# Two attention blocks with a gate: mask products of the maxima issued ahead, and three small tasks moved by one group

## The chip, the cores and the metric

The kernel runs on one core of a Trainium2 chip. The metric is the device time of one execution in microseconds (us). A core has five engines that run side by side: TensorE (in the profile PE, and PEld for its weight loads), VectorE (DVE), ScalarE (ACT), GpSimd (POOL) and SyncE (SP), which issues the transfers. TensorE writes its products into eight banks of a small memory, PSUM, from which VectorE and ScalarE read them.

## The reference

Two attention blocks read the same input of 2048 positions and 512 columns, with 32 heads of 16 columns each, and a gate mixes their outputs.

```python
def _A_ref(x, wq, wk, wv, wo, beta):          # 4 chunks of 512 positions
    ...
    for s in range(N):
        qs, ks, vs = q[:, :, s], k[:, :, s], v[:, :, s]
        logits = jnp.einsum("bhqd,bhkd->bhqk", qs, ks) * scale + mask   # causal inside the chunk
        p = _softmax(logits, axis=-1)
        a_dot = jnp.einsum("bhqk,bhkd->bhqd", p, vs)
        pq = phi(qs)
        num = jnp.einsum("bhld,bhde->bhle", pq, M)
        den = jnp.einsum("bhld,bhd->bhl", pq, z)[..., None] + 1e-6
        outs.append(g * (num / den) + (1.0 - g) * a_dot)
        M = M + jnp.einsum("bhld,bhle->bhde", phi(ks), vs)
        z = z + ...
    ...
def _B_ref(x, wqkv, wo):                      # every position sees all 2048
    scores = jnp.einsum("bhqd,bhkd->bhqk", q, k) * (Dh ** -0.5)
    p = _softmax(scores, axis=-1)
    o = jnp.einsum("bhqk,bhkd->bhqd", p, v)
    ...
g = _sigmoid((x * gate_w).sum(-1, keepdims=True))
return g * a + (1 - g) * b
```

The softmax of both blocks subtracts the maximum of a row, and the kernel computes these maxima in passes of their own.

## The kernel before

**Units and rounds.** Work is cut into units: a unit is four heads and one chunk of 512 queries. Block A has 32 (numbers 0 to 31), block B has 32 (32 to 63). After a first stage of about 400 us (projections, the memory of block A, first maxima) come 32 rounds. Round `k` works on unit `32 + k` of B and unit `k` of A.

**Slots.** A round has 37 groups, here called slots: `n` from 0 to 31 for B (16 key tiles, two heads at a time), 32 to 36 for A. All instructions of a slot are issued in the order in which the loop over `n` calls the functions, and each engine runs its own in that order. A slot holds:

- `t_group`: products of keys and queries (line 503, on half of the rows of TensorE each, two side by side) into two of the three banks TB0, TB1 and MB, the least recently used first; then two exponentials on ScalarE (line 509), and in A's slots a masking of the diagonal on GpSimd (line 512).
- the tasks of `plan`: maxima of units that come later. A task writes logits into SBK (two pairs of banks, taken in turn by `rot("s", SBK)`), and VectorE takes the maximum over the keys.
- `pvs`: products of probabilities and values (`pv`, line 525) into the one bank PVB, for groups issued earlier. In slot 33 the last of them for B's unit, and behind it a copy of the bank by `fin_copy` (on ScalarE for B, line 534); in slot 34 the first of A's unit, into the same bank. In slot 36 two calls for A, in slot 0 of the next round A's last one and a copy on VectorE (line 532).
- in some slots `beside`, with the finishing of earlier units. In slot 36 of every even round from 8 on, `out_split` (ScalarE line 584, GpSimd line 585). In slot 1 of the rounds from 9 on, `out_mm` (24 products, line 591).

**The tasks.** Each round computes the maxima of one later unit of B in 32 tasks (`s_b`: two products, line 449, reduction in line 451) and of the next unit of A in 6 (`s_a`, in the order of `ST_A`). A's tasks take the query tiles 3, 3, 2, 2, 1, 0; the first four have one pair of heads each (one part), the last two have both (two parts, in the columns 0 to 255 and 256 to 511 of a bank). A part is one product of queries and keys for each of the two row halves (line 427), followed by two small products for each half that add the causal mask (line 431: `crows` as weights, `cmask` streaming, 128 and 64 columns wide). The reductions are in lines 435 and 437.

**Where the tasks stand.** `spread` puts one B task into each of the slots 20 to 31 and 36 of a round and 1 to 19 of the next; A's tasks stand in the slots 32 to 36 and, the sixth, in slot 0 of the next round. So slot 36 has two tasks, A's fifth and one of B. `m_chain` in slot 21 reads the maxima.

Of the kernel before, what the change touches and what calls it, by code (L numbers as in the profile page):

```python
# [23 lines left out]
NT = SEQ // 128  # L24
# [3 lines left out]
S_FIRST = 10  # L28
S_LAST = 10
# [4 lines left out]
def gated_mix_kernel(ctx, tc, x, wq, wk, wv, wo, beta, wqkv, wob, gate_w, out):  # L34
    nc = tc.nc
# [16 lines left out]
    cmask = P.tile([128, 2, 128], BF, name="cmask")  # L52
    crows = P.tile([128, 2, 128], BF, name="crows")
# [31 lines left out]
    SBK = [PS.tile([128, 2, C], FT, name=f"sbk{i}") for i in range(2)]  # L85
    lru = []

    def bank(allowed):
        b = min(allowed, key=lambda a: max([n for n, x in enumerate(lru) if x is a], default=-1))
        lru[:] = [x for x in lru if x is not b] + [b]  # L90
        return b
# [17 lines left out]
    def rot(key, lst):  # L109
        i = cnt.get(key, 0)  # L110
        cnt[key] = i + 1
        return lst[i % len(lst)]
# [262 lines left out]
    def q_of(u):  # L375
        return QA[u % 2] if u < 32 else QB[u % 3]

    def k_of(u, p):
        return KA[u % 2][:, p] if u < 32 else KB[(u - 32) % 3][:, p]
# [18 lines left out]
    def load_vb(g):  # L398
        v_src(VB[g % 2], "B", g % 4, None)
# [8 lines left out]
    def pair_max(k):  # L408
        if k not in MX:
            MX[k] = W.tile([128, 2, 4, 4], FT, name="mx")  # L410
        return MX[k]

    def chain_of(u):

        return u + 1 if u else 0

    def s_a(u, i, p):
        mx = pair_max(chain_of(u))
        n = 128 * (i + 1)
        b = rot("s", SBK)  # L420
        todo_p = [(0, p)] if p is not None else [(0, 0), (256, 1)]
        for c0, p in todo_p:
            for n2 in range(3):
                for j in (1, 0):
                    r = slice(64 * j, 64 * j + 64)
                    if n2 == 0:
                        nc.tensor.matmul(b[:, j, c0:c0 + n], q_of(u)[r, p, i * 128:(i + 1) * 128], k_of(u, p)[r, :n],  # L427
                                         start=True, stop=False)
                    else:
                        w = 192 - 64 * n2  # L430
                        nc.tensor.matmul(b[:, j, c0 + n - w:c0 + n], crows[r, n2 - 1], cmask[r, n2 - 1, 128 - w:],  # L431
                                         start=False, stop=n2 == 2)
        m = mx[:, 0].rearrange("q (j p) i -> q j p i", j=2)
        if len(todo_p) == 1:
            nc.vector.tensor_reduce(m[:, :, p, i], b[:, :, :n], axis=AX.X, op=OP.max)  # L435
        else:
            nc.vector.tensor_reduce(m[:, :, :, i], b.rearrange("q j (p k) -> q j p k", p=2)[:, :, :, :n], axis=AX.X,
                                    op=OP.max)
# [52 lines left out]
    def t_group(u, n, banks):  # L491


        kd, qd, c = UN[u]
        bs = [bank(banks) for _ in range(2)]
        c0 = 0
        for it, hs in (((n // 2, (n % 2 * 2, n % 2 * 2 + 1)),) if kd == "B" else GA[n]):
            q0 = 128 * it if kd == "A" else 0
            w = C - q0
            pn = it if kd == "B" else it % 2  # L500
            for j, h in enumerate(hs):
                r = slice(64 * j, 64 * j + 64)
                nc.tensor.matmul(bs[j][:, c0:c0 + w], k_of(u, h // 2)[r, 128 * it:128 * it + 128],  # L503
                                 q_of(u)[r, h // 2, q0:], start=True, stop=True)
                PT[u, it, h] = PTILE[pn % 2][:, 2 + j if (kd, it) == ("A", 2) else h][:, c0:c0 + w]
            c0 += w
        for j in range(2):
            pt = PTILE[pn % 2][:, 2 + j if (kd, n) == ("A", 4) else hs[j]]
            nc.scalar.activation(pt, bs[j], AF.Exp, scale=SCALE)  # L509
            if kd == "A":  # L510
                m = pt[:, :128] if n < 2 else pt.rearrange("p (a t) -> p a t", a=4)[:, ::3 if n < 4 else 2]
                nc.gpsimd.affine_select(out=m, in_=m, pattern=[[1, 128]] if n < 2 else [[0, 2], [1, 128]],  # L512
                                        compare_op=OP.is_ge, fill=0.0, base=0, channel_multiplier=-1)
# [119 lines left out]
    def todo(fn, *a):  # L633
        return lambda: fn(*a)
# [87 lines left out]
    for blk in range(16):  # L722
# [10 lines left out]
        n = blk + 1 + (c == 2)  # L733
# [74 lines left out]
    def late():  # L808
        proj.close()
        L = AT["L"] = ctx.enter_context(tc.tile_pool(name="late", bufs=1))  # L810
        VB[1] = L.tile([128, NT, 8, E + 1], FT, name="vb1")
        AT["o"] = [L.tile([128, 4, 2, C], FT, name=f"o{n}") for n in range(2)]
        AT["wh"] = L.tile([128, 4, 2, DM], FR, name="wh")
        AT["wl"] = L.tile([128, 4, 2, DM], FR, name="wl")
        AT["d"] = [L.tile([128, C], FT, name=f"d{n}") for n in range(2)]
        AT["oh"] = L.tile([128, 4, 2, 128], FR, name="oh")
        AT["ol"] = L.tile([128, 4, 2, 128], FR, name="ol")
        for p in range(2):
            set_aux(KB[2][:, p], 0)

    T3 = TB + [MB]
    TAIL = T3 + [SBK[0][:, 0]]
    mode["misc"] = T3
    NG = 2 * NT + 5

    def pvs(k, n):

        ua, ub = k, 32 + k
        if n == 0:
            if k:  # L830
                pv(ua - 1, 2)
                fin_copy(ua - 1)
        elif k == 31 and n < 2 * NT:
            if n % 2 and n > 1:
                pv(ub, n // 2 - 1)
        elif 2 <= n < 2 * NT + 2:
            pv(ub, n // 2 - 1, n % 2 * 256, n % 2 * 256 + 256)
            if n == 2 * NT + 1:
                fin_copy(ub)
        elif n > 2 * NT + 1:  # L840
            m = n - 2 * NT - 2
            if m < 2:
                pv(ua, 0, 256 * m, 256 * m + 256)
            else:
                pv(ua, 1)
                pv(ua, 3)

    def extras(k):

        pre, post = {}, {}  # L850
        if not k:
            for n in range(4):
                pre[2 * n] = [fill[n - 4]]
        post[2 * S_LAST + 4] = [todo(m_rows, k + 1)]
        for n, at in [(k - 9, 1)] + [(23, 2 * OMI)] * (k == 31):
            if n >= 0:
                pre[at] = [todo(out_mm, n // 8, n // 2 % 4, n % 2)]
        return pre, post
# [28 lines left out]


    ex = [extras(k) for k in range(32)]
    plan = {}  # L890

    def spread(tasks, gs):
        for n, p in enumerate(gs):
            plan.setdefault(p, []).extend(tasks[len(tasks) * n // len(gs):len(tasks) * (n + 1) // len(gs)])

    for k in range(31):
        if k:
            spread([todo(s_b, 33 + k, *t) for t in (sorted(ST_B, key=lambda t: t[2]) if k == 1 else ST_B)],
                   [(k - 1, n) for n in list(range(2 * S_FIRST, 2 * NT)) + [NG - 1]] + [(k, n) for n in range(1, 2 * S_LAST)])
        else:  # L900
            spread(st33[EARLY:], sorted([(0, n) for n in range(2 * S_LAST)] + [(0, 2 * n) for n in range(4)]))
        for n, t in enumerate(ST_A):
            plan.setdefault((k, 2 * NT + n) if n < 5 else (k + 1, 0), []).append(todo(s_a, k + 1, *t))

    for k in range(32):
        ua, ub = k, 32 + k
        banks = T3 + [b[:, 0] for b in SBK] * (k == 31)
        for n in range(NG):
            it = n // 2 if n < NG - 1 else NT + 2
            t_group(*(ub, n) if n < 2 * NT else (ua, n - 2 * NT), banks)  # L910
            for f in plan.get((k, n), []) + ex[k][0].get(n, []):
                f()
            pvs(k, n)
            for f in ex[k][1].get(n, []):
                f()
            if n % 2 == 0 and n < NG - 1:
                continue
            beside(k, it)
            if it == S_LAST:
                m_chain(k + 1)  # L920
            if it == 4 and not k:
                late()
            if it == 4 and not k:
                load_q(ub + 2)
                for c in range(NC4):
                    load_kb(2, c)
            if it == NT and k < 29:
                load_q(ub + 3)
                load_kb(k + 3)
            if it == 6 and k < 31:  # L930
                load_q(ua + 1)
                load_ka(ua + 1)
                if (ua + 1) % 2 == 0:
                    load_va(ua + 1)
            if it == 9:
                if k % 2 == 0 and k < 30:
                    load_vb(k // 2 + 1)
                if 1 <= k <= 4:
                    load_wo(k - 1)
# [55 lines left out]
```

## Time and profile before

| | |
|---|---|
| median of 3 runs | 1983.9 us (1976.98, 1983.9, 1985.88) |
| profiled execution | span 1976.0 us from the first to the last instruction; no time of its own is listed beside it |
| instructions | 43643 |
| TensorE busy | 1944.8 us (98%) |
| VectorE busy | 1630.3 us (83%) |
| ScalarE busy | 1435.7 us (73%) |
| GpSimd busy | 257.5 us (13%) |
| mean granted TensorE clock | 0.997 |
| transfers | 222.49 MB, mean 113 GB/s |

Busy TensorE is modelled: products are pipelined, so a busy engine isn't an engine at its peak. In the timeline a row has the start in us, the length in us, the engine, the line, the operation, the tiles (written <- read) with the shape, how many instructions it merges, and in brackets how long the engine had been idle and what ended that.

### The profile page before, as it was taken

The page shows a single profiled execution, that of the slowest core. Times are in us where ns is not written, and L with a number is a line of the kernel's source. Part 1 is how long each engine was busy: PE and PEld are TensorE (multiplying, and loading weights), DVE is VectorE, ACT ScalarE, POOL GpSimd, SP SyncE. Part 2 cuts the span into 40 slices and gives each one's busy share as a digit, 9 for nine tenths or more (in the row PEclk, how much of TensorE's full clock was granted, in tenths as well). Part 3 has the DMA queues.
Part 4 walks back from the last instruction along what each step waited for, and adds up shares of the span by engine and source line. Part 5 has one row for each costly group of instructions (what it writes and reads, how often), then busy time and mean ns, then how long its engine had stood idle before and what let it go on. Part 6 is the DMA issues. An engine that isn't in the chain of part 4 may idle for free.

```text
span 1976.0 us, 43643 instructions
## 1 busy us (share of the span) xinstructions
PE 1944.8 (98%) x17517; PEld 945.6 (48%) x17517; DVE 1630.3 (83%) x1825; ACT 1435.7 (73%) x2703; POOL 257.5 (13%) x474
## 2 busy tenths in 40 slices
PE   8999999999999999999999999999999999999999
PEld 6887777434344344444444444444444444444435
DVE  6135665899999999999999999999999999999942
ACT  3233332688888888888888888888888888888884
POOL 2200000011210101111010101010101010101012
PEclk9999999999999999999999999999999999999999
DMA  6766656644443444344445353444344444444111
GB/s 205 172 209 183 191 186 173 152 111 114 97 114 88 103 86 103 86 114 86 114 85 112 86 113 86 114 86 114 86 108 91 96 102 87 102 90 103 48 51 57
DMA packets 162742, 222.49 MB, mean 113 GB/s; under 512 B 39260, under 2 KB 89452, under 8 KB 156780
## 3 DMA queue, kind: packets, MB, share of 16 engines
q1 hardware_dynamic: 159596, 211.70, 44.0%
q0 software_dynamic: 2944, 8.00, 2.1%
q8 instruction: 138, 2.26, 0.5%
q14 instruction: 64, 0.52, 0.1%
HBM read 148.21 MB, written 68.16 MB: 109 GB/s over the span
## 4 chain that ended last, share of the span: by engine, by line
PE 90%; DMA 3%; DVE 2%; ACT 2%; issue 1%; SPq 1%; ACTq 0%; DVEq 0%
PE pvb L525 31%; PE tb L503 17%; PE sbk L449 12%; PE mb L503 8%; PE tb L279 3%; PE tb L591 2%; PE mb L279 2%; PE sbk L427 2%; PE pvb L279 2%; PE tb L262 2%; DVE mxb L451 1%; ACT raw L509 1%; PE mb L591 1%; PE mb L262 1%; PE sbk L431 1%
## 5 line engine op out<-in xcount | busy, mean ns | idle before, releaser
L451 DVE TENSOR_REDUCE mxb<-sbk 128x2 f32<-128x1024 f32 x1024 | 1226.1, 1222 | 36.6 <-PE sbk L449 32.4
L509 ACT ACTIVATE raw<-tb 128x512 f32<-128x512 f32 x1557 | 888.2, 598 | 163.1 <-PE tb L503 90.7
L525 PE MATMUL pvb<-raw,vb 128*17 128x256 f32 (+1 forms) x8072 | 639.4, 388 | 0.0
L509 ACT ACTIVATE raw<-mb 128x512 f32<-128x512 f32 x780 | 466.4, 598 | 76.5 <-PE tb L503 44.8
L503 PE MATMUL tb<-qb,xh 64*128 64x512 f32 x872 | 330.8, 496 | 1.7 <-ACT raw L509 1.7
L525 PEld LDWEIGHTS pvb<-raw,vb 128*17 128x17 f32 x8072 | 134.4, 95 | 341.7 <-issue 336.6
L449 PE MATMUL sbk<-xh,qb 64*128 64x512 f32 x1344 | 283.1, 398 | 2.0 <-DMA xh<-dB 0.8
L503 PE MATMUL mb<-qb,xh 64*128 64x512 f32 x445 | 219.6, 494 | 0.0
L503 PEld LDWEIGHTS tb<-qb,xh 64*128 64x128 f32 x872 | 124.4, 183 | 188.1 <-issue 91.4
L512 POOL TENSOR_SCALAR_AFFINE_SELECT raw<-raw 128x256 f32<-128x256 f32 (+1 forms) x320 | 116.1, 363 | 700.1 <-ACT raw L509 692.3
L503 PE MATMUL tb<-qb,kb 64*128 64x512 f32 x471 | 176.3, 496 | 1.4 <-DMA qb<-mr 0.8
L435 DVE TENSOR_REDUCE mx<-sbk 128x2 f32<-128x768 f32 (+1 forms) x128 | 139.8, 1092 | 43.1 <-PE sbk L431 37.1
L449 PE MATMUL sbk<-kb,qb 64*128 64x512 f32 x704 | 150.6, 406 | 1.2 <-DVE mxb L451 1.1
L449 PEld LDWEIGHTS sbk<-xh,qb 64*128 64x128 f32 x1344 | 137.9, 186 | 7.3 <-DVE mxb L451 3.5
L503 PEld LDWEIGHTS mb<-qb,xh 64*128 64x128 f32 x445 | 81.3, 183 | 86.6 <-issue 48.0
L503 PE MATMUL mb<-qb,kb 64*128 64x512 f32 x233 | 115.4, 495 | 0.7 <-DVE st L289 0.7
L565 POOL TENSOR_TENSOR o<-o,d 128x512 f32<-128x512 f32 x31 | 39.8, 1283 | 562.6 <-DMA d<-rd 281.6
L503 PEld LDWEIGHTS tb<-qb,kb 64*128 64x128 f32 x471 | 66.0, 183 | 98.4 <-issue 52.5
L525 PE MATMUL pvb<-raw,va 128*17 128x256 f32 (+2 forms) x1280 | 94.7, 383 | 5.8 <-ACT pvs L534 5.8
L427 PE MATMUL sbk<-ka,qa 64*128 64x256 f32 (+3 forms) x512 | 86.8, 346 | 1.2 <-ACT raw L509 1.2
L503 PE MATMUL tb<-qa,ka 64*128 64x384 f32 (+3 forms) x340 | 79.2, 372 | 0.0
L449 PEld LDWEIGHTS sbk<-kb,qb 64*128 64x128 f32 x704 | 71.6, 185 | 12.6 <-issue 6.5
(273 smaller groups left out, 1790.7 us busy)
## 6 DMA issues: line engine op xcount, KB each, us to landing
xh<-dB SPq DMA_DIRECT2D x38, 512.0 KB
vb<-vdB SPq DMA_DIRECT2D x16, 1088.0 KB
dB<-st SPq DMA_DIRECT2D x64, 256.0 KB
dA<-st SPq DMA_DIRECT2D x64, 256.0 KB
pd<-pvs SPq DMA_DIRECT2D x64, 256.0 KB
kb<-dB SPq DMA_DIRECT2D x22, 512.0 KB
xh<-dB SPq DMA_DIRECT2D x38, 256.0 KB
qb<-dB SPq DMA_DIRECT2D x64, 128.0 KB
```

The source lines that it names most:

```text
L262: nc.tensor.matmul(b, lhs, WV[wi][:, k, :], start=n == 0, stop=n == 11)
L279: nc.tensor.matmul(b, WS[ws][w][wi][:, k, :], (XH, XL)[xi][c][:, k, :], start=n == 0, stop=n == 11)
L427: nc.tensor.matmul(b[:, j, c0:c0 + n], q_of(u)[r, p, i * 128:(i + 1) * 128], k_of(u, p)[r, :n], start=True, stop=False)
L435: nc.vector.tensor_reduce(m[:, :, p, i], b[:, :, :n], axis=AX.X, op=OP.max)
L449: nc.tensor.matmul(b[:, j], q_of(u)[r, p, i * 128:(i + 1) * 128], k_of(u, p)[r, kc * C:(kc + 1) * C], start=True, stop=True)
L451: nc.vector.tensor_reduce(MXB[u][:, :, p, i, kc], b, axis=AX.X, op=OP.max)
L503: nc.tensor.matmul(bs[j][:, c0:c0 + w], k_of(u, h // 2)[r, 128 * it:128 * it + 128], q_of(u)[r, h // 2, q0:], start=True, stop=True)
L509: nc.scalar.activation(pt, bs[j], AF.Exp, scale=SCALE)
L512: nc.gpsimd.affine_select(out=m, in_=m, pattern=[[1, 128]] if n < 2 else [[0, 2], [1, 128]], compare_op=OP.is_ge, fill=0.0, base=0, channe ...
L525: nc.tensor.matmul(PVB[32 * h:32 * h + E + 1, q0 + lo:q0 + hi], vt[:, it, 4 * q + h, :], pt[:, lo:hi], start=it == 0 and lo == 0, stop=it ...
L565: nc.gpsimd.tensor_tensor(o, o, d, op=OP.mult)
L591: nc.tensor.matmul(b, (AT["oh"], AT["ol"])[oi][:, g, a], (AT["wh"], AT["wl"])[wi][:, g, a], start=n == 0, stop=n == 11)
```

## The change

Three things are changed.

1. The products of A's maxima. The mask products of a task come first and open the accumulation (`start`), the products with the keys follow and close it. A task with two parts issues the masks of both parts, then its products with the keys. The masks are issued by a function of their own, `s_mask`, which also takes the bank.
2. In each of the slots 32 to 36 the masks of the slot's first A task are issued at the head of the slot, ahead of `t_group`; its products with the keys stay behind `t_group`. A second A task in a slot issues its masks right ahead of its own products.
3. The order. A's fourth, fifth and sixth task move up by one slot (to 34, 35 and 36), so slot 34 holds the third and the fourth. The B task of slot 36 moves to slot 0 of the next round. In slot 0 of round 31 `t_group` may no longer use the SBK banks.

```diff
@@ -414,22 +414,34 @@
+    SA = {}
+
+    def parts_of(p):
+        return [(0, p)] if p is not None else [(0, 0), (256, 1)]
+
+    def s_mask(u, i, p):
+        n = 128 * (i + 1)
+        b = SA[u, i, p] = rot("s", SBK)
+        for c0, _ in parts_of(p):
+            for n2 in range(2):
+                w = 128 - 64 * n2
+                for j in (1, 0):
+                    r = slice(64 * j, 64 * j + 64)
+                    nc.tensor.matmul(b[:, j, c0 + n - w:c0 + n], crows[r, n2], cmask[r, n2, 128 - w:],
+                                     start=c0 == 0 and n2 == 0, stop=False, skip_group_check=True)
+
     def s_a(u, i, p):
+        if (u, i, p) not in SA:
+            s_mask(u, i, p)
         mx = pair_max(chain_of(u))
         n = 128 * (i + 1)
-        b = rot("s", SBK)
-        todo_p = [(0, p)] if p is not None else [(0, 0), (256, 1)]
-        for c0, p in todo_p:
-            for n2 in range(3):
-                for j in (1, 0):
-                    r = slice(64 * j, 64 * j + 64)
-                    if n2 == 0:
-                        nc.tensor.matmul(b[:, j, c0:c0 + n], q_of(u)[r, p, i * 128:(i + 1) * 128], k_of(u, p)[r, :n],
-                                         start=True, stop=False)
-                    else:
-                        w = 192 - 64 * n2
-                        nc.tensor.matmul(b[:, j, c0 + n - w:c0 + n], crows[r, n2 - 1], cmask[r, n2 - 1, 128 - w:],
-                                         start=False, stop=n2 == 2)
+        b = SA.pop((u, i, p))
+        todo_p = parts_of(p)
+        for c0, h in todo_p:
+            for j in (1, 0):
+                r = slice(64 * j, 64 * j + 64)
+                nc.tensor.matmul(b[:, j, c0:c0 + n], q_of(u)[r, h, i * 128:(i + 1) * 128], k_of(u, h)[r, :n],
+                                 start=False, stop=(c0, h) == todo_p[-1], skip_group_check=True)
...
-    plan = {}
+    plan, lead = {}, {}
...
-                   [(k - 1, n) for n in list(range(2 * S_FIRST, 2 * NT)) + [NG - 1]] + [(k, n) for n in range(1, 2 * S_LAST)])
+                   [(k - 1, n) for n in range(2 * S_FIRST, 2 * NT)] + [(k, n) for n in range(2 * S_LAST)])
...
         for n, t in enumerate(ST_A):
-            plan.setdefault((k, 2 * NT + n) if n < 5 else (k + 1, 0), []).append(todo(s_a, k + 1, *t))
+            at = (k, 2 * NT + n - (n > 2))
+            lead.setdefault(at, todo(s_mask, k + 1, *t))
+            plan.setdefault(at, []).append(todo(s_a, k + 1, *t))
 
     for k in range(32):
         ua, ub = k, 32 + k
-        banks = T3 + [b[:, 0] for b in SBK] * (k == 31)
         for n in range(NG):
+            banks = T3 + [b[:, 0] for b in SBK] * (k == 31 and n > 0)
             it = n // 2 if n < NG - 1 else NT + 2
+            if (k, n) in lead:
+                lead[k, n]()
             t_group(*(ub, n) if n < 2 * NT else (ua, n - 2 * NT), banks)
```

## The prediction

> **What bounds the kernel now.** I read the page first, then the timeline of one late round, engine by engine. The page:
>
> ```profile
> span 1976.0 us, 43643 instructions
> PE 1944.8 (98%) x17517; PEld 945.6 (48%) x17517; DVE 1630.3 (83%) x1825; ACT 1435.7 (73%) x2703; POOL 257.5 (13%) x474
> PE 90%; DMA 3%; DVE 2%; ACT 2%; issue 1%; SPq 1%; ACTq 0%; DVEq 0%
> ```
>
> The chain that ended last is TensorE for 90% of the span: its queue sets the time, and another engine matters only where TensorE waits for it. So every edit is priced as microseconds in TensorE's order. The page gives the profiled execution no time besides its span; the lowest of the three runs, 1976.98, is 1.0 us above it, and the median 6.9 us above that. I add the change that I find to the median.
>
> TensorE's rows of the timeline give the steps. T is the product of a probability group (line 503), K a product with the keys for a maximum (427, and 449 for B), M a mask product (431), PV line 525. First two groups (slots) with a B task, then A's slots 32 and 33:
>
> ```profile
> 988.46 0.52 PE L503 MATMUL tb<-qb,kb 64*128 64x512 f32 x2
> 988.80 0.42 PE L449 MATMUL sbk<-xh,qb 64*128 64x512 f32 x2
> 989.14 0.63 PE L525 MATMUL pvb<-raw,vb 128*17 128x256 f32 x8
> 989.70 0.50 PE L503 MATMUL mb<-qb,kb 64*128 64x512 f32 x1
> ...
> 990.04 0.39 PE L449 MATMUL sbk<-xh,qb 64*128 64x512 f32 x2
> 990.36 0.62 PE L525 MATMUL pvb<-raw,vb 128*17 128x256 f32 x8
> 990.92 0.50 PE L503 MATMUL tb<-qa,ka 64*128 64x512 f32 x1
> ...
> 991.28 0.46 PE L427 MATMUL sbk<-ka,qa 64*128 64x512 f32 x2
> 991.51 0.33 PE L431 MATMUL sbk<-cmask,crows 64*128 64x128 bf16 x4
> 991.78 0.63 PE L525 MATMUL pvb<-raw,vb 128*17 128x256 f32 x8
> 992.33 0.50 PE L503 MATMUL tb<-qa,ka 64*128 64x512 f32 x2
> 992.67 0.40 PE L427 MATMUL sbk<-ka,qa 64*128 64x512 f32 x2
> 992.91 0.26 PE L431 MATMUL sbk<-cmask,crows 64*128 64x128 bf16 x4
> 993.10 0.63 PE L525 MATMUL pvb<-raw,vb 128*17 128x256 f32 x8
> 993.65 0.44 PE L503 MATMUL mb<-qa,ka 64*128 64x384 f32 x1
> ```
>
> From start to start: T to K 0.34, K to PV 0.33, PV to the next T 0.56; a B slot is 1.22 to 1.24. Slot 33 is 1.32 (T to K 0.34, K to M 0.24, M to PV 0.19, PV to T 0.55): the four small masks of one part cost 0.10. Slot 32 is 1.41; its two row halves are out of step. The rest of A's slots, and slots 0 and 1 of the next round:
>
> ```profile
> 994.00 0.39 PE L427 MATMUL sbk<-ka,qa 64*128 64x384 f32 x2
> 994.23 0.26 PE L431 MATMUL sbk<-cmask,crows 64*128 64x128 bf16 x4
> 994.64 0.63 PE L525 MATMUL pvb<-raw,va 128*17 128x256 f32 x8 [0.16 <-ACT pvs L534]
> 995.20 0.44 PE L503 MATMUL tb<-qa,ka 64*128 64x384 f32 x1
> ...
> 996.52 0.50 PE L503 MATMUL tb<-qa,ka 64*128 64x256 f32 x4
> 996.86 0.27 PE L427 MATMUL sbk<-ka,qa 64*128 64x256 f32 x2
> 996.97 0.26 PE L431 MATMUL sbk<-cmask,crows 64*128 64x128 bf16 x4
> 997.07 0.36 PE L427 MATMUL sbk<-ka,qa 64*128 64x256 f32 x2
> 997.27 0.26 PE L431 MATMUL sbk<-cmask,crows 64*128 64x128 bf16 x4
> 997.37 0.48 PE L449 MATMUL sbk<-xh,qb 64*128 64x512 f32 x2
> 997.78 1.06 PE L525 MATMUL pvb<-raw,va 128*17 128x384 f32 x16
> 998.77 0.50 PE L503 MATMUL mb<-qb,xh 64*128 64x512 f32 x1
> ...
> 1000.15 0.49 PE L503 MATMUL tb<-qb,xh 64*128 64x512 f32 x1
> ```
>
> Slots 32 to 36 and 0 take 1.41, 1.32, 1.55, 1.32, 2.25 and 1.38: 9.23 us from 990.92 to 1000.15, in each of the 31 rounds with A tasks. All that the change can win or lose lies in here. Slot 36 holds two tasks, A's fifth and a B task. Slot 34 has TensorE's one clear wait: M to PV is 0.41 where slot 33 has 0.19, a loss of 0.22, until ScalarE has copied the PV bank of B's unit.
>
> **What is removed.** Call A's six tasks A0 to A5. The change puts A3 into slot 34 beside A2, A4 into 35, A5 into 36, and the B task of slot 36 into slot 0. Slot 0 becomes a plain B slot: 1.38 to 1.22, a gain of 0.16. In slot 34, A3's work stands where TensorE waited 0.22. The number of products, and all DMAs and queues but TensorE's and VectorE's order, stay.
>
> **What the moved masks cost.** No row shows a mask behind PV and ahead of T. Nearest is the part inside slot 36: 996.97 to 997.07, 0.10. I take 0.12 for a first part ahead of T (its weights come right behind PV, where nothing hides them) and 0.22 for two (A4 and A5 have two). Bounds: nothing net, if T's own weight load runs under the masks; 0.27, as from 991.51 to 991.78 with the row halves out of step. And K without masks behind it goes to PV in 0.33 instead of 0.24 and 0.19, 0.10 less. So slot 33 becomes 0.12 + 0.34 + 0.33 + 0.56 = 1.35 by rounded rows, 1.32 by the unrounded ones: nothing is won there. Slot 32 wins about 0.06 as its halves run in step.
>
> Does T get its weights earlier behind masks? K of 256 columns behind M takes 0.20 to the next step (997.07 to 997.27), behind T only 0.11 (996.86 to 996.97): 0.09 of weight load stays open behind a mask. So I leave T to K at 0.34. The Trainium skill's "TensorE: Matmul & The Clock Gate" ("Step-by-step: what each phase is for") says that TensorE pulls weight loads ahead of running products while the products stay in program order. By its first half T's load would vanish under the masks (the fast rival below); the 0.20 row disagrees for short masks. Its second half is the danger: a mask that waits for its bank holds T behind it.
>
> **The new waits.** The two SBK banks alternate, so a task's mask waits for VectorE to have reduced the task two before it. Until now that wait came behind T; now it comes ahead of T, with T, ScalarE's exponentials and GpSimd's masks queued behind. VectorE's rows, GpSimd's and ScalarE's:
>
> ```profile
> 989.26 2.44 DVE L451 TENSOR_REDUCE mxb<-sbk 128x2 f32<-128x1024 f32 x2
> 996.08 0.96 DVE L435 TENSOR_REDUCE mx<-sbk 128x2 f32<-128x768 f32 x1 [0.59 <-PE sbk L431]
> 1000.45 0.68 DVE L532 COPY pvs<-pvb 128x512 f32<-128x512 f32 x1
> 996.46 0.90 POOL L512 TENSOR_SCALAR_AFFINE_SELECT raw<-raw 128x256 f32<-128x256 f32 x2 [0.51 <-ACT raw L509]
> 997.11 1.08 ACT L509 ACTIVATE raw<-tb 128x512 f32<-128x512 f32 x2 [0.23 <-PE tb L503]
> 998.08 1.06 ACT L584 ACTIVATE oh<-o 128x1024 fp32r<-128x1024 f32 x1
> 999.30 0.60 ACT L509 ACTIVATE raw<-mb 128x512 f32<-128x512 f32 x1 [0.16 <-PE tb L503]
> ```
>
> A reduction starts about 0.45 after its K (988.80 to 989.26), and takes 1.22 or, for A2 and A3, 0.96. Count from the first mask of slot 32. Slots 32 and 33 take 1.35 and 1.32, so slot 34 begins at 2.67. T follows at 2.79 and A2's K at 3.13 (0.12 and 0.35 on). A3's mask needs A1's bank, whose K stood at 1.81: reduced at 1.81 + 0.45 + 1.22 = 3.48. A3 then takes 0.10 for its masks and 0.36 for K and the way into PV (0.26 as behind a mask at 997.07, and 0.10 more), so PV stands at about 3.97, by when the copy is done. A2's bank is reduced at 3.13 + 0.45 + 0.96 = 4.54. A4's mask needs that bank, ahead of T of slot 35; TensorE itself would be there at 3.97 + 0.56 = 4.53. So this wait is small but it is the path: T of slot 35 comes at 4.54 + 0.04 + 0.22 = 4.80. From T to the PV that reads its masked exponentials there pass 2.2 (995.20 to the end of GpSimd's row, 996.46 + 0.90 = 997.36, and a little for the semaphore). TensorE's own work up to PV of slot 36 would be about 2.1 now, since the B task is gone: it waits. PV at 7.00, T of slot 0 at 7.99 (0.99 on, 997.78 to 998.77), T of slot 1 at 9.21 with the 1.22 of a plain slot. Today the same stretch is 9.23. **The sum of a round is a gain of 0.02**, with 0.16 and 0.22 gained and eaten by A3's own work and the two new waits.
>
> On top, slot 36 is shorter, and ScalarE's 1.06 us of line 584 (rounds 8, 10 to 30: 12 of them) ends later against slot 0. T of slot 36 comes at about 6.3; today line 584 starts 1.56 behind it (996.52 to 998.08), so it would run from 7.9 to 8.9. The first exponential of slot 0, which starts 0.53 behind T (998.77 to 999.30), would be ready at 8.5 but wait until 8.85; its bank, needed by T of slot 1, comes free 0.6 later, at 9.5 instead of 9.2. That is 0.3 x 12 = 3.6 us lost. In all: -31 x 0.02 + 3.6 = +3 us; I take +1, as half of these delays may be absorbed where out_mm follows in slot 1: **1985 us**.
>
> The B task in slot 0 puts a 1.22 reduction ahead of VectorE's copy in place of one of 0.68, so slot 1's reduction starts some 0.6 late. Its bank is needed two slots on, 2.44 after its K, and 0.45 + 1.22 of that are used: 0.77 of cover remains, and the lag is smaller. Without cover the price would be at most the 0.6 in 8 early rounds, 5 us. The order inside tasks before round 0 is off this path, and the bank list of slot 0 in round 31 is one slot: nothing for both.
>
> **Rivals.** *Fast:* T's weight load runs under the leading masks. T to K then falls from 0.34 to about 0.23 in slots 32 to 35, 0.4 a round on the path above, 13 us: **1972**. For it: weights load beside products all over the trace (PEld is busy 48%). Against: the 0.20 row. *Slow:* a leading part costs more than 0.12, because masks, T and K no longer run into one another. Five parts lie on the path (slots 32, 33, 34, and two in 35), priced at 0.58 in all. At the 0.27 of slot 32 they cost 1.35, 0.77 more a round, 24 us: **2009**; halfway 1997. It decides, past 0.5%, from about 0.18 a part. Against it: three of the four orders of neighbours that it needs stand in the trace, at 0.10. *Not as it says:* if the masks' bank always came free late, "ahead" would be only a wait; in slots 32 and 33 the bank is reduced long before (B tasks' reductions end at 990.5 and 991.7), so this holds at most in slot 35, and is in the sum.
>
> **How the numbers follow.** The three runs spread by 0.45%, so about 0.5%, 9.9 us, is what a measurement here can tell from no change. My forecast has 0.60, with its own range 1977 to 1992; the fast rival 0.18, the slow one 0.22. The range takes the fast rival in almost whole and half of the slow one's reach: 1969 to 2000. Faster by over 0.5% is the fast rival, slower the slow one, and within 0.5% the forecast.
>
> **What would show it.** Right: slots 32 and 33 of the new profile unchanged within 0.05; slot 34's PV without a wait for the copy; slot 35's masks starting just behind A2's reduction; a wait for GpSimd ahead of PV in slot 36; slot 0 at 1.22; in every second late round a wait of T in slot 1 for an exponential. Wrong: T to K clearly under 0.3 behind masks, parts at 0.2 or more, or B slots off 1.22 to 1.24.

## The result, and the profile after

| | before | after |
|---|---|---|
| median of 11 runs (lowest to highest) | 1978.79 us (1976.2 to 1985.88) | 1988.85 us (1985.2 to 1994.3) |
| span of the profiled execution | 1976.0 us | 1984.3 us |

The ratio is 1.0042, 95% interval 1.0031 to 1.0054: slower by 0.4%, some 8 us, and by the ratio within the 0.5% of the forecast. The medians themselves are 10.1 us apart, 0.51%, so it lies at the edge. But two things of opposite sign stand in it, and the larger one I had priced at nothing.

The page of the changed kernel says little. TensorE is as busy as before, and holds 94% of the chain that ended last instead of 90%:

```profile
span 1984.3 us, 43595 instructions
PE 1949.8 (98%) x17517; PEld 942.5 (47%) x17517; DVE 1629.2 (82%) x1825; ACT 1436.2 (72%) x2703; POOL 256.7 (13%) x474
PE 94%; DMA 2%; DVE 2%; ACT 1%; SPq 1%; issue 0%; POOL 0%; ACTq 0%; DVEq 0%
```

What helps is to cut both timelines at the first T of each round and compare piece by piece. All pieces are worked out from the starts of T's rows. Where a slot's length is given from here on for all rounds, it is the median over the rounds 9 to 29, from T to T (so a mask ahead of T counts to the slot before). The first T comes at 349 us, so the first stage is shorter than the 400 us given above.

| piece, us | before | after | change |
|---|---|---|---|
| up to the first T of round 0 | 349.3 | 348.3 | -1.1 |
| rounds 0 to 30 | 1553.9 | 1548.2 | -5.8 |
| mean of rounds 9 to 29: even, odd | 50.37, 50.30 | 50.09, 50.27 | -0.28, -0.03 |
| round 31, first T to last T | 43.5 | 59.0 | **+15.5** |
| from there to the end | 29.3 | 28.9 | -0.4 |
| sum (the span) | 1976.0 | 1984.3 | +8.3 |

The rounds in which the change does its work got faster. How much is less certain than the table looks: up to round 31 x1 below has the instructions of the changed kernel, and x2 and x7 have those of the kernel before. Their profiled executions reach the first T of round 31 at 1899.8 (x1), 1902.2 (x2) and 1902.7 (x7), where the table gives 1896.4 after and 1903.2 before. So the gain up to there is 2.4 to 6.8 us, 4.6 in the mean. The rounds 9 to 29 agree far better (50.18 and 50.20 against 50.33 to 50.34), and their 0.14 times 31 rounds would be 4.4.

The whole loss is in round 31, which in the changed kernel has no maxima to compute at all. First a round with A tasks, TensorE's rows from the masks of slot 32 (986.95) to slot 1 of the next round (line 430 is the masks, 443 A's K, 515 T, 537 PV):

```profile
986.95 0.26 PE L430 MATMUL sbk<-cmask,crows 64*128 64x128 bf16 x4
...
988.25 0.26 PE L430 MATMUL sbk<-cmask,crows 64*128 64x128 bf16 x4
988.34 0.48 PE L515 MATMUL tb<-qa,ka 64*128 64x512 f32 x2
988.66 0.39 PE L443 MATMUL sbk<-ka,qa 64*128 64x512 f32 x2
988.98 0.62 PE L537 MATMUL pvb<-raw,vb 128*17 128x256 f32 x8
989.54 0.26 PE L430 MATMUL sbk<-cmask,crows 64*128 64x128 bf16 x4
...
989.95 0.39 PE L443 MATMUL sbk<-ka,qa 64*128 64x384 f32 x2
990.37 0.26 PE L430 MATMUL sbk<-cmask,crows 64*128 64x128 bf16 x4
990.45 0.43 PE L443 MATMUL sbk<-ka,qa 64*128 64x384 f32 x2
990.82 0.63 PE L537 MATMUL pvb<-raw,va 128*17 128x256 f32 x8
991.39 0.35 PE L430 MATMUL sbk<-cmask,crows 64*128 64x128 bf16 x8
991.56 0.42 PE L515 MATMUL mb<-qa,ka 64*128 64x384 f32 x1
...
993.60 1.21 PE L537 MATMUL pvb<-raw,va 128*17 128x384 f32 x16
994.73 0.50 PE L515 MATMUL mb<-qb,xh 64*128 64x512 f32 x1
...
995.95 0.50 PE L515 MATMUL tb<-qb,xh 64*128 64x512 f32 x1
996.16 0.50 PE L515 MATMUL mb<-qb,xh 64*128 64x512 f32 x1
```

A leading part costs 0.09 (988.25 to 988.34), two parts 0.17 (991.39 to 991.56), and T to K takes 0.32 behind masks. The wait for the copy ahead of PV in slot 34 is gone; A3's masks stand there, 0.42 behind A2's K (989.95 to 990.37). From the first mask to T of slot 1 pass 9.00 us (986.95 to 995.95), where the kernel before needed 9.23. The last two rows are one T: its second half comes 0.21 late. ScalarE's rows show why:

```profile
993.59 1.09 ACT L521 ACTIVATE raw<-tb 128x512 f32<-128x512 f32 x2 [0.35 <-PE tb L515]
994.56 1.06 ACT L596 ACTIVATE oh<-o 128x1024 fp32r<-128x1024 f32 x1
995.50 0.60 ACT L521 ACTIVATE raw<-mb 128x512 f32<-128x512 f32 x1
```

The exponential of slot 0 starts 0.77 behind its T (994.73 to 995.50) where it used to start 0.53 behind; the copy of line 596 (584 before) ran until 995.6. This happens in every second round.

Now round 31. TensorE's rows of the kernel before, then of the changed one:

```profile
1911.09 0.50 PE L503 MATMUL tb<-qb,xh 64*128 64x512 f32 x1
1911.09 0.73 PE L503 MATMUL sbk<-qb,xh 64*128 64x512 f32 x2
1911.67 0.49 PE L503 MATMUL mb<-qb,xh 64*128 64x512 f32 x1
1912.09 1.10 PE L525 MATMUL pvb<-raw,vb 128*17 128x512 f32 x8
1913.12 0.51 PE L503 MATMUL tb<-qb,xh 64*128 64x512 f32 x2
```

```profile
1904.13 0.50 PE L515 MATMUL sbk<-qb,xh 64*128 64x512 f32 x2
1905.31 0.98 PE L515 MATMUL sbk<-qb,xh 64*128 64x512 f32 x2 [0.69 <-ACT raw L521]
1906.22 1.05 PE L537 MATMUL pvb<-raw,vb 128*17 128x512 f32 x8
1907.20 0.49 PE L515 MATMUL sbk<-qb,xh 64*128 64x512 f32 x2
1908.38 0.98 PE L515 MATMUL sbk<-qb,xh 64*128 64x512 f32 x2 [0.68 <-ACT raw L521]
```

Read the tile column. Before, T writes tb, mb and sbk in turn, and two slots take 2.03 here (1911.09 to 1913.12) and 1.96 in most pairs of the round. After, every T from slot 1 on writes sbk, two products and the same two banks each time; the next T must wait until ScalarE has read them, and two slots take 3.07 (1904.13 to 1907.20). Who waited for whom in round 31 of the changed kernel, summed:

```profile
PEld sbk L515 <- ACT raw L521: 33.4, 50, 1.1
...
ACT raw L521 <- PE sbk L515: 14.6, 17, 2.3
...
PE sbk L515 <- ACT raw L521: 9.0, 14, 0.7
```

The first row is idle time of the weight loads; the products themselves waited for the 9.0 us of the last. TensorE and ScalarE wait for each other in turn, as with one buffer.

### The profile page after: what moved, and what is told of

The parts are those of the page before. It is cut to its first block, busy times and chain, and to the rows that moved or that the text cites. A ratio compares the mean times of both kernels' runs of the same rounds, so it can differ in the third digit from the quotient of the medians.

```text
span 1984.3 us, 43595 instructions
## 1 busy us (share of the span) xinstructions
PE 1949.8 (98%) x17517; PEld 942.5 (47%) x17517; DVE 1629.2 (82%) x1825; ACT 1436.2 (72%) x2703; POOL 256.7 (13%) x474
## 3 DMA queue, kind: packets, MB, share of 16 engines
q8 instruction: 138, 2.26, 0.5%
## 4 chain that ended last, share of the span: by engine, by line
PE 94%; DMA 2%; DVE 2%; ACT 1%; SPq 1%; issue 0%; POOL 0%; ACTq 0%; DVEq 0%
PE pvb L537 33%; PE tb L515 17%; PE sbk L461 12%; PE mb L515 8%; PE tb L279 3%; PE tb L603 2%; PE sbk L443 2%; PE sbk L430 2%; PE mb L279 2%; PE pvb L279 2%; PE tb L262 2%; PE sbk L515 1%; PE mb L603 1%; PE mb L262 1%; PE sbk L279 1%; DVE mxb L463 1%
## 5 line engine op out<-in xcount | busy, mean ns | idle before, releaser
L521 ACT ACTIVATE raw<-tb 128x512 f32<-128x512 f32 x1529 | 870.8, 596 | 161.5 <-PE tb L515 93.0
L521 ACT ACTIVATE raw<-mb 128x512 f32<-128x512 f32 x767 | 457.2, 596 | 72.8 <-PE tb L515 31.6
L515 PE MATMUL tb<-qb,xh 64*128 64x512 f32 x848 | 322.1, 496 | 1.7 <-ACT raw L521 1.7
L515 PE MATMUL mb<-qb,xh 64*128 64x512 f32 x434 | 214.6, 495 | 0.0
L537 PE MATMUL pvb<-raw,va 128*17 128x256 f32 (+2 forms) x1280 | 99.1, 384 | 0.3 <-ACT pvs L546 0.2
L443 PE MATMUL sbk<-ka,qa 64*128 64x256 f32 (+3 forms) x512 | 78.1, 337 | 0.0
L515 PE MATMUL tb<-qa,ka 64*128 64x512 f32 (+3 forms) x334 | 74.1, 357 | 0.0
```

What stands on the lines that cost most here:

```text
L443: nc.tensor.matmul(b[:, j, c0:c0 + n], q_of(u)[r, h, i * 128:(i + 1) * 128], k_of(u, h)[r, :n], start=False, stop=(c0, h) == todo_p[-1], s ...
L537: nc.tensor.matmul(PVB[32 * h:32 * h + E + 1, q0 + lo:q0 + hi], vt[:, it, 4 * q + h, :], pt[:, lo:hi], start=it == 0 and lo == 0, stop=it ...
```

## The experiments

The theory came from the code beside these rows. The choice of the least recently used bank compares bank objects by identity (`x is a`). The kernel before made the list `[b[:, 0] for b in SBK]` once a round. The change moved that line into the loop over slots, to leave out slot 0, so each slot makes new view objects (Python objects that stand for part of a bank), which the record of used banks doesn't know: both SBK banks look never used, and are always taken. The rival was that the placement itself costs the time: no SBK in slot 0, or banks that come free at another moment.

**The views made once in the changed kernel (x1).** `S0` is a list of the same two views that exists already.

```diff
-            banks = T3 + [b[:, 0] for b in SBK] * (k == 31 and n > 0)
+            banks = T3 + S0 * (k == 31 and n > 0)
```

> The changed kernel, but the two bank views of SBK are made once and reused in round 31, instead of anew in each slot. Theory (views): the least-recently-used choice compares objects by identity, so views made anew in every slot always look unused and every T of round 31 goes into the same two banks; the trace of the changed kernel shows round 31 from its first T to its last at 59.0 us against 43.5. Then round 31 falls back to about 43.5, the gain of rounds 0 to 30 (6.8 us in the traces) stays, and the kernel is 6 to 8 us under the kernel before, ratio 0.996 to 0.997. Rival (late banks): round 31 is long because slot 0 may not use SBK and the moved A task frees its bank at another time; then this kernel stays at about 8 us over the kernel before, ratio 1.004.

Measured: ratio 0.9955 (0.9943 to 0.9968), median 1972.6 us. Round 31 takes 41.8 us from its first T to its last, rounds 9 to 29 are 50.20 on average (50.11 even, 50.28 odd). Both the ratio and round 31 are a little lower than expected (0.996 to 0.997, and 43.5). The rival is out. Three banks and more are in use again:

```profile
1904.32 0.50 PE L515 MATMUL mb<-qb,xh 64*128 64x512 f32 x1
1904.33 0.49 PE L515 MATMUL tb<-qb,xh 64*128 64x512 f32 x1
1904.66 0.39 PE L515 MATMUL sbk<-qb,xh 64*128 64x512 f32 x2
1904.99 1.05 PE L537 MATMUL pvb<-raw,vb 128*17 128x512 f32 x8
1905.97 0.50 PE L515 MATMUL tb<-qb,xh 64*128 64x512 f32 x1
```

**The views made anew in the kernel before (x2).** Nothing else is touched.

```diff
-        banks = T3 + [b[:, 0] for b in SBK] * (k == 31)
         for n in range(NG):
+            banks = T3 + [b[:, 0] for b in SBK] * (k == 31)
```

> The kernel before, with nothing changed but that the bank list of round 31 is made anew in each slot. Theory (views): round 31 grows by about 15 us in the trace, the other rounds stay within 1 us, ratio 1.0075 to 1.008. Rival (late banks): no task is moved here, so the time stays as before, ratio 1.000.

Measured: ratio 1.0098 (1.0083 to 1.0114). Round 31 takes 62.6 us instead of 43.5, rounds 9 to 29 stay at 50.34. The theory holds from the other side too, with the same pattern in the rows:

```profile
1911.61 0.99 PE L503 MATMUL sbk<-qb,xh 64*128 64x512 f32 x2 [0.74 <-ACT raw L509]
1912.53 1.05 PE L525 MATMUL pvb<-raw,vb 128*17 128x512 f32 x8
1913.51 0.50 PE L503 MATMUL sbk<-qb,xh 64*128 64x512 f32 x2
```

The loss is larger than I said, 19.1 us. The fair comparison is x1 against the changed kernel, where the new views cost 17.2 (59.0 less 41.8). The last section says where 1.4 us of the remaining 1.9 are.

**The 2 by 2: leading masks and moved tasks (x1, x3, x4, x6).** With the views made once, x3 leaves the leading out, x4 the moved tasks, x6 both (masks first inside the task is left). All keep the rule for slot 0 of round 31.

```diff
x3, x6:
-            if (k, n) in lead:
-                lead[k, n]()
x4, x6:
-            at = (k, 2 * NT + n - (n > 2))
+            at = (k, 2 * NT + n) if n < 5 else (k + 1, 0)
(and the B task back in slot 36, as before)
```

> As x1, but no masks go ahead of T: every task issues its masks right ahead of its own products with the keys. The order of tasks is the changed one. What it tells apart is how the gain of rounds 0 to 30 is shared. If the moved tasks bring it (the wait for the copy in slot 34 filled, slot 0 a plain slot), the ratio is 0.996 to 0.998, like x1 or up to 1.5 us more. If the leading masks bring it (they run into T for 0.10 a part), most of the 7 us is lost and the ratio is 0.999 to 1.000. From the rows I expect slots 32 and 33 at about 1.32 to 1.34 instead of 1.29 to 1.30.

> As x1, but the order of tasks is that of the kernel before (A's fifth beside a B task in slot 36, the sixth in slot 0): masks first and ahead of T only. If the moved tasks bring the gain, slot 34 keeps its wait for the copy of about 0.2 and slot 0 stays near 1.38, and the ratio is 0.998 to 1.000. If the leading masks bring it, the ratio is near 0.997. The masks of the sixth task stand ahead of T in slot 0; a ratio over 1.000 would say that leading masks alone cost time.

> The fourth cell of two by two: masks first inside the task, but neither ahead of T nor with moved tasks (bank views made once). x3 shows masks between T and K: T to M 0.34, M to K 0.10, K to PV 0.41, so slot 33 at 1.41 against 1.32 before and 1.29 with leading masks. If this holds by itself, slots 32 to 36 and 0 cost 0.05 to 0.1 each more than before, rounds 9 to 29 average about 50.6, and with the 1.7 us gained in round 31 the ratio is 1.002 to 1.005. If the loss in x3 came from the moved tasks, the rounds stay at 50.34 and the ratio is 0.999.

| rounds 9 to 29, mean us (ratio, interval) | tasks as before | tasks moved |
|---|---|---|
| masks behind T | x6: 50.29 (0.9968, 0.9957 to 0.9979) | x3: 50.36 (0.9980, 0.9967 to 0.9993) |
| masks ahead of T | x4: 50.19 (0.9973, 0.9961 to 0.9986) | x1: 50.20 (0.9955, 0.9943 to 0.9968) |
| the kernel before | 50.34 | |

The intervals of the four overlap or nearly do, so I read the rounds' lengths and not the ratios. Leading is worth 0.10 with the old order and 0.16 with the new one. Moving the tasks is worth nothing on average: 0.07 lost without leading, 0.01 with it. With leading, the 0.01 is a gain and a loss: even rounds take 50.11 in x1 and 50.21 in x4, odd ones 50.28 and 50.17, for the late copy stands in the odd rounds of x1. The expectation of x3 would have read its ratio of 0.998 as a gain of the moved tasks; by the rounds it is not, 1.9 us of it are in round 31. Its slots 32 and 33 take 1.42 and 1.40, not 1.32 to 1.34. Of x6 the bound was wrong: masks first gained 0.05 where I expected a loss of 0.3. In x6 slot 33 is longer as expected (1.40), but slot 34 is 1.47 (1.55 before), since its masks run while PV would wait for the copy, and slot 36 with its two parts 2.15 (2.26 before). What leading saves shows in the rows of x3, slot 33:

```profile
995.18 0.50 PE L515 MATMUL tb<-qa,ka 64*128 64x512 f32 x2
995.52 0.26 PE L430 MATMUL sbk<-cmask,crows 64*128 64x128 bf16 x4
995.62 0.48 PE L443 MATMUL sbk<-ka,qa 64*128 64x512 f32 x2
996.03 0.63 PE L537 MATMUL pvb<-raw,vb 128*17 128x256 f32 x8
996.59 0.44 PE L515 MATMUL mb<-qa,ka 64*128 64x384 f32 x1
```

Behind a mask K takes 0.41 to PV, behind T 0.32. I read the 0.09 as weight load of K that a short mask does not hide, but that is not shown: T right behind a mask shows no such loss, it takes 0.32 to K (988.34 to 988.66) and 0.34 behind PV. The slot is 1.41 with masks between T and K, 1.32 before (K, then masks), 1.29 with masks ahead of T. In x4 the wait that the moved tasks were to fill is still there, and larger, since less work stands ahead of it:

```profile
993.92 0.39 PE L443 MATMUL sbk<-ka,qa 64*128 64x384 f32 x2
994.61 0.63 PE L537 MATMUL pvb<-raw,va 128*17 128x256 f32 x8 [0.29 <-ACT pvs L546]
```

That filling it wins nothing on average is what the prediction said: A3's masks beside A2 come 0.42 behind K, and in every second round the late copy takes 0.2.

**Slot 0 of round 31 (x7).** x1, x3, x4 and x6 all spend 41.6 to 42.3 us on round 31, less than the 43.5 of the kernel before. x7 is the kernel before with that rule alone, views made once.

```diff
-        banks = T3 + [b[:, 0] for b in SBK] * (k == 31)
         for n in range(NG):
+            banks = T3 + S0 * (k == 31 and n > 0)
```

> The kernel before, but T of slot 0 in round 31 may not use SBK (the views are made once). In the kernel before this T waits 0.34 for VectorE and the A task behind it 1.17 for an exponential, in the same banks. Theory: these waits are what x1, x3 and x4 gain in round 31, 43.5 to 41.6 to 42.0; then this kernel has 41.6 to 42.2 there, nothing changes elsewhere, and the ratio is 0.999. Rival: round 31 is shorter because the last A task has moved or has its masks first; then it stays at 43.5 and the ratio is 1.000.

Measured: round 31 at 42.3, rounds 9 to 29 at 50.33, ratio 0.9980 (0.9966 to 0.9994). So 1.2 us of the 1.7 that x1 gains in round 31 are this rule. The other 0.5 are in the slots 0 and 1, which take 1.38 and 3.66 in x7 and 1.02 and 3.52 in x1: there x1 has no A task in slot 0, since it has moved. The ratio of x7 amounts to 4 us, more than the 1.2 that the round explains, and elsewhere its products are those of the kernel before; so ratios that differ by no more than this 0.1 or 0.2% tell little. Rows of the kernel before with the waits that the rule removes:

```profile
1903.25 0.50 PE L503 MATMUL sbk<-qb,xh 64*128 64x512 f32 x2 [0.34 <-DVE mx L437]
1904.92 0.33 PE L427 MATMUL sbk<-ka,qa 64*128 64x128 f32 x2 [1.17 <-ACT raw L509]
```

**The late copy (x5).** x1, with the copy of `out_split` on VectorE.

```diff
-        nc.scalar.activation(AT["oh"], o_cols(c, t), AF.Copy)
+        nc.vector.tensor_copy(AT["oh"], o_cols(c, t))
```

> As x1, but the copy of line 584 (out_split, in slot 36 of every even round from 8 on) runs on VectorE instead of ScalarE. Theory (late copy): in x1 the even rounds take 50.11 and the odd ones 50.28, because that ScalarE copy ends after the exponential of the next slot 0 is ready and holds T of slot 1 by 0.2. Without it on ScalarE the odd rounds fall to about 50.1 as well, some 2 us in all, ratio 0.994 to 0.995, and T of slot 1 no longer comes in two parts. Rival: odd rounds are longer for another reason (the output products stand in both kinds of rounds, but the loads differ), then they stay at 50.28; or VectorE falls behind by the copy and its banks come late, then slots 1 to 3 grow and the ratio is 0.996 or more.

Measured: ratio 0.9958 (0.9943 to 0.9973), not to be told from x1. In the odd rounds slot 1 falls from 3.81 to 3.61, as the theory says, and T there comes in one piece again. But slot 0 grows from 1.22 to 1.34, and the odd rounds only fall from 50.28 to 50.23. GpSimd's rows of the diagonal masks of slot 36, in x5 and in x1:

```profile
994.81 1.22 POOL L524 TENSOR_SCALAR_AFFINE_SELECT raw<-raw 128x256 f32<-128x256 f32 x2 [0.54 <-ACT raw L521]
```

```profile
997.51 0.90 POOL L524 TENSOR_SCALAR_AFFINE_SELECT raw<-raw 128x256 f32<-128x256 f32 x2 [0.54 <-ACT raw L521]
```

While VectorE copies beside them (0.89 us from 994.88), the two selects take 1.22 instead of 0.90, and A's last PV in slot 0 needs them: from it to the next T pass 0.68 us (995.95 to 996.63) instead of 0.56. It is the second select alone that is longer, 0.73 instead of 0.41, in all 12 rounds with the copy and in none of the others from 9 to 29. The late copy is shown as the cause of the 0.2 in slot 1; taking it off ScalarE handed 0.12 of it back through GpSimd.

## Why the prediction was right, and where it was wrong

- **The total** was within the half per cent by the ratio, and the measured time, 1988.85, is inside the forecast's own range of 1977 to 1992. A good part of that is luck. The forecast started from a median of 1983.9 over three runs, which is 1978.8 over eleven; read as a change, its range was -7 to +8 us, and the measured change is +8 by the ratio and +10 by the medians. And two misses cancel in part: +15.5 us from a step that it set at nothing, and -6.8 us up to round 31 (4.6 in the mean of all traces) where its sum had +3.
- **The step that failed** is the sentence "the bank list of slot 0 in round 31 is one slot: nothing for both". I read what the condition `n > 0` does, and not what moving the line into the loop does. x1 and x2 show its price: removing it from the changed kernel takes 17 us off round 31, adding it to the kernel before puts 19 us on.
- **The path of a round** held in most of its steps. Slot 34 started at 2.59 (2.67 forecast), its length was 1.85 (1.87), A4's masks came at 4.44 (4.54 forecast for the bank), T of slot 0 at 7.78 (7.99), T of slot 1 at 9.00 (9.21). A3's mask did wait for A1's reduction: A2's K to the masks took 0.42 where 0.23 stood before. It came 0.05 behind the end of that reduction (990.32 to 990.37), and A4's masks as much behind A2's (991.34 to 991.39), in all rounds from 9 to 29. The second wait is nearly nothing, as forecast: the masks stand 0.57 behind PV, where the other slots have 0.55 or 0.56. The wait for GpSimd in slot 36 was there, but inside PV: 1.13 to the next T (993.60 to 994.73) instead of 0.99. And T of slot 35 to that PV took 2.04 (991.56 to 993.60) where 2.2 was forecast.
- **Mis-sized terms.** A leading part costs 0.09 and not 0.12, two cost 0.17 and not 0.22. T to K is 0.32 behind masks and not 0.34, so of the 0.11 that the fast rival needed at most 0.02 is there. Slot 32 fell from 1.41 to 1.30, more than the 0.05 that the forecast allowed it. Together a round gains 0.23 in place of 0.02, ahead of the late copy.
- **The late copy** was right as a mechanism: every second round loses 0.2, where 0.3 was forecast.
- **The moved tasks** gained on average no more than the waits that they bring, as forecast; x3 against x6, and x1 against x4, show it. The slow rival (parts at 0.18 or more) is refuted by the 0.09, the copy wait in slot 34 went, slot 0 became 1.22, and the B slots stayed at 1.22 to 1.24.

Without the slip in round 31 the change is a gain: x1 beats both kernels, by 0.45% against the one before. That is 9 us, of which the two profiled executions show 5.2 (spans of 1976.0 and 1970.8).

## What to carry to other kernels

Cut two timelines at the same landmark and compare piece by piece before explaining a sum: here a small gain in each of 31 rounds and a larger loss in the one round that the change hardly touches added up to a small number. When a line moves into a loop, ask what it creates there; a chooser that compares by identity forgets everything it knew, and the tile column of the profile shows that at once (the same bank in every row). And try small products in each place that the order allows: here the same four masks made the slot 1.29 ahead of the group, 1.32 behind the two long products and 1.41 between them.

## What the runs showed of the hardware that I had not expected

- What masks cost the long product behind them is not always the same: K takes 0.41 to PV behind masks and 0.32 behind T, while T takes 0.32 to K behind masks and 0.34 behind PV. Why the two differ is not shown.
- GpSimd's two selects took 1.22 us instead of 0.90 beside a VectorE copy of 128x1024 elements, and the first of them was not slower.
- In x2 the granted clock fell for a few microseconds of round 31, just behind a stretch with two waits of TensorE, 0.34 and 1.17 long. Two windows there, each with its length, the busy times of PE, PEld, DVE, ACT and POOL, the clock, the DMA share and the GB/s. Below them stands the same stretch of the kernel before, with the same two waits:

```profile
1902.00:1905.80 3.80, 2.42 (x24) 1.21 (x24) 1.29 (x3) 1.74 (x4) 2.36 (x2) 1.00 0.12 35
1905.80:1910.40 4.60, 4.60 (x15) 3.36 (x14) 4.43 (x11) 0.92 (x2) 0.00 (x0) 0.63 0.21 63
```

```profile
1903.05:1906.85 3.80, 2.43 (x25) 1.33 (x26) 1.29 (x3) 1.73 (x4) 2.37 (x2) 1.00 0.12 34
1906.85:1911.45 4.60, 4.60 (x27) 2.60 (x25) 4.43 (x11) 2.81 (x6) 0.00 (x0) 1.00 0.20 64
```

With 0.63 of the clock the 12 output products took 4.5 us from the first to the next T, where the changed kernel took 3.1 at a granted clock of 1.00: these are the 1.4 us. The Trainium skill ("TensorE: Matmul & The Clock Gate", "What's actually happening") says that a window of idleness of about 3.4 us brings the clock to half. Here TensorE was busy for 2.42 of the 3.80 us ahead, so the drop agrees with the rule only if a partly idle window is enough. But the kernel before was busy for 2.43 of 3.80 us in the same place and kept a clock of 1.00. The waits alone therefore do not explain the drop, and its cause stays open.
